# First input tile in halves on two queues, alternating loads, delayed products: a start-up change to a linear-attention kernel

## The chip, the cores and the metric

One core of one Trainium2 chip. The metric is the device time of one execution in microseconds (us). Several executions of each kernel are run and the median is quoted. The profile's span is about 2 us shorter than the time and comes from one execution.

The engines in the profile: PE is the TensorE matmul, PEld its weight load, DVE is VectorE, ACT is ScalarE, POOL is GpSimd, SP is SyncE. SP and ACT each own a DMA queue here.

## The reference

Two linear-attention blocks A and B read the same input x (2048 rows, 640 columns, bf16), each with its own weights, and a gate per row mixes their results.

```
g = sigmoid((x * gate_w).sum(-1))
q, k, v = split(x @ wqkv)              # 32 heads of 20
phi = lambda t: where(t > 0, t + 1, exp(t)) + 1e-6
kv = einsum(phi(k), v);  z = phi(k).sum(over rows)
o  = (phi(q) @ kv) / (phi(q) @ z + 1e-6)
block = o @ wo
out = g * block_A + (1 - g) * block_B
```

## The kernel before

The kernel is a list of operations that a small scheduler in Python orders on each engine, with a semaphore for each dependency. Four parts matter here. A "tile" is 128 rows of x; a "chunk" is 128 of the 640 rows of a weight matrix.

The loads that the first products need: input tiles 0 to 3 and the five chunks of A's key weights, 160 KB each.

```
load_wk("ACT", 0)
load_x("SP", 0)
load_wk("ACT", 1)
load_x("SP", 1)
load_wk("ACT", 2)
load_wk("SP", 3)
load_wk("ACT", 4)
load_x("SP", 2)
load_x("ACT", 3)
# ... then all else, on SP
```

The order on PE at the start. Everything up to the fourth block of key products is chained, so PE runs it in exactly this order. `warm` is a dummy matmul of 512 columns, `transpose_x(t)` is five PE transposes and one copy by DVE from PSUM to SBUF, and `first("A", (t, c))` is the two 320-column products of tile t with chunk c.

```
warm(7)
transpose_x(0)
warm(1)
transpose_x(1)
first("A", (0, 0), (0, 1))
warm(1)
first("A", (1, 0), (1, 1))
first("A", (0, 2), (1, 2), (0, 3), (1, 3))
transpose_x(2)
# ... (0, 4), (1, 4), transpose_x(3), then all of tiles 2 and 3
```

The middle: query products, with the small products `wp_unit("B", q)` (masked inner matrix times output weights) strewn between them. `wp_unit` needs a mask that DVE applies to the result of `m_unit`.

```
def queries(b):
    for X in XS:
        for k in range(NC):
            q_unit(X, b, k)
            if b == 1 and X == "A":
                wp_unit("B", k)
queries(0)
m_unit("B", 0)
m_unit("B", 1)
queries(1)
wp_unit("B", 5)
```

The denominators: DVE adds epsilon to them, then takes the reciprocal.

```
sch.op("DVE", lambda e: e.tensor_scalar(DN[...], PS[...], EPS, None, op0=ALU.add), ...)
```

Of the kernel before, what the change touches and what calls it, by code (L numbers as in the profile page):

```python
# [24 lines left out]
NC = 5  # L25
EPS = 1e-6
HALF = 320
XW = 672
PE_GHZ = 2.4

# [276 lines left out]
def _dve_ns(n, rate=1):  # L307
    return n / (0.96 * rate) + 68.0
# [6 lines left out]
def bass_gated_mix__linear_attn_block__linear_attn_block__prompt_kernel(nc, A_x, A_wqkv, A_wo, B_x, B_wqkv, B_wo, gate_w, out):  # L315
# [6 lines left out]
    with ExitStack() as es:  # L322
        E = es.enter_context

        def sb(name, shape, dtype=dt.bfloat16):
            return E(nc.sbuf_tensor(name, shape, dtype))
# [24 lines left out]
        GWB = sb("GWB", [128, D])  # L351
        NTS = 3
        TS = sb("TS", [128, NTS, D], dt.float32)
        DN = sb("DN", [128, 2, 256], dt.float32)
        RC = sb("RC", [128, 2, 256])
        RX = sb("RX", [128, 2, 1024])
# [32 lines left out]
        def mms(name, steps, reads, writes, cols, lat=190.0, par=1, prio=None, after=None):  # L389


            def fn(pe):
                ins = None
                for o, l, r, a, z, tp in steps():
                    ins = pe.matmul(o, l, r, start=a, stop=z, tile_position=tp, skip_group_check=True)  # L395
                return ins

            return sch.op("PE", fn, cols / PE_GHZ / par, reads=reads, writes=writes, name=name, lat=lat, prio=prio, after=after)
# [5 lines left out]
            return weights(X, lo, 0, NC)  # L404


        sch.op("POOL", lambda e: e.memset(IDN[:, :], 0.0), 150, writes=[("ID",)], name="id0")
        sch.op(
            "POOL",
# [8 lines left out]
        def load_x(eng, t):  # L418
            dma(eng, "xn%d" % t, XN[:, t, 0:D], xin[128 * t : 128 * t + 128, :], writes=[("XN", t)], us=0.25)

        def load_wk(eng, c):
            dma(eng, "wkA%d" % c, WK["A"][:, c, :], weights("A", D, c, c + 1)[:, 0, :], writes=[("WK", "A", c)], us=0.25)

        load_wk("ACT", 0)
        load_x("SP", 0)
        load_wk("ACT", 1)
        load_x("SP", 1)
        load_wk("ACT", 2)
        load_wk("SP", 3)
        load_wk("ACT", 4)  # L430
        load_x("SP", 2)
        load_x("ACT", 3)
        for c0, c1 in ((0, 1), (1, 3), (3, 5)):
            dma(
                "SP", "wkB%d" % c0, WK["B"][:, c0:c1, :], weights("B", D, c0, c1), writes=[("WK", "B", c) for c in range(c0, c1)],
# [38 lines left out]
        def transpose_x(t):  # L474
            tt = _Tile(1)

            def fn(pe):
                ins = None
                for c in range(NC):
                    ins = pe.transpose(PSB[:, tt.banks[0], 128 * c : 128 * c + 128], XN[:, t, 128 * c : 128 * c + 128], IDN[:, :])  # L480
                return ins

            at[0] = sch.op(
                "PE", fn, 5 * 112, reads=[("XN", t), ("ID",)], writes=[(tt,)], name="xpose%d" % t, lat=190, after=at[0]
            )
            sch.op(
                "DVE",
                lambda e: e.tensor_copy(
                    XT[:, :, 128 * t : 128 * t + 128], PSB[:, tt.banks[0], 0:D].rearrange("p (c f) -> p c f", f=128)
                ),  # L490
                _dve_ns(D), reads=[(tt,)], writes=[("XT", t)], name="xev%d" % t,
            )

        ring = {"ek": _Ring(NEK), "dn": _Ring(2), "rx": _Ring(2), "os": _Ring(NOS), "ts": _Ring(NTS)}

# [26 lines left out]
        def k_part(X, t, tile, cs, chain=False):  # L522
            xc = slice(128 * t, 128 * t + 128)
            order = [(h, c) for h in (0, 1) for c in cs] if len(cs) == NC else [(h, c) for c in cs for h in (0, 1)]

            def steps():
                return [
                    (PS[:, tile.banks[h], 0:HALF], XT[:, c, xc], WK[X][:, c, HALF * h : HALF * h + HALF], c == 0, c == NC - 1, None)
                    for h, c in order
                ]  # L530

            o = mms(
                "k%s%d_%d" % (X, t, cs[0]), steps, [("XT", t)] + [("WK", X, c) for c in cs], [(tile,)], len(cs) * (D + 12),
                after=at[0] if chain else None,
            )
            if chain:
                at[0] = o
# [142 lines left out]
        def q_unit(X, b, k):  # L680
            tile = _Tile(1)
            es = _Tile(1, ring["ek"])

            def ek():
                return EK[:, es.slot, 0:512]

            dst = PQ[X][:, k, 512 * b : 512 * b + 512]
            span = range(S * k + 512 * b, S * k + 512 * b + 512)
            over = [("F", X, "k", t) for t in range(span[0] // D, span[-1] // D + 1)]

            def steps():
                return [
                    (PS[:, tile.banks[0], :], WQ[X][:, c, k : D : NC], XT[:, c, 512 * b : 512 * b + 512], c == 0, c == NC - 1, None)
                    for c in range(NC)
                ]

            mms("q%s%d%d" % (X, b, k), steps, [("XT", t) for t in range(4 * b, 4 * b + 4)] + [("WQ", X)], [(tile,)], NC * 518, after=gone[X])
            sch.op(
                "ACT", lambda e: e.activation(ek(), PS[:, tile.banks[0], :], ACT.Exp), _act_ns(512), reads=[(tile,)],  # L699
                writes=[(es,)], name="eq%s%d%d" % (X, b, k),  # L700
            )
            sch.op(
                "DVE", lambda e: e.tensor_scalar(ek(), ek(), 1.0, EPS, op0=ALU.min, op1=ALU.add), _dve_ns(512, 4),  # L703
                reads=[(es,)], writes=[(es,)], name="tq%s%d%d" % (X, b, k),
            )
            sch.op(
                "DVE",
                lambda e: e.scalar_tensor_tensor(  # L708
                    out=dst, in0=PS[:, tile.banks[0], :], scalar=0.0, in1=ek(), op0=ALU.max, op1=ALU.add
                ),  # L710
                _dve_ns(512), reads=[(tile,), (es,)], writes=[("PQ", X, k, b)] + over, name="sq%s%d%d" % (X, b, k),
            )
# [24 lines left out]
        def scale_q(b, dtile, pieces):  # L737

            ds = _Tile(1, ring["dn"])
            lo = 256 * (b % 2)  # L740
            sch.op(
                "DVE",
                lambda e: e.tensor_scalar(DN[:, ds.slot, :], PS[:, dtile.banks[0], lo : lo + 256], EPS, None, op0=ALU.add), _dve_ns(256),
                reads=[(dtile,)], writes=[(ds,)], name="dn%d" % b,
            )

            def rec(e):
                with nc.allow_low_precision(reason="the factor is a bf16 matmul operand"):
                    return e.reciprocal(RC[:, ds.slot, :], DN[:, ds.slot, :])

            sch.op("DVE", rec, 1740, reads=[(ds,)], writes=[(ds,)], name="rc%d" % b)
            rep = FD[b].ap()
            dma(
                "SP", "fw%d" % b, rep.rearrange("g h r f -> (g h) r f"), lambda: RC[:, ds.slot, :].unsqueeze(1).to_broadcast([128, 4, 256]),
                reads=[(ds,)], writes=[("FD", b)], us=0.6,
            )
            xs = _Tile(1, ring["rx"])
            dma(
                "SP", "fr%d" % b, lambda: RX[:, xs.slot, :].rearrange("p (g f) -> p g f", f=256), rep.rearrange("g h r f -> (h r) g f"),
                reads=[("FD", b)], writes=[(xs,)], us=0.6,  # L760
            )
            w = 512 // pieces
            for j in range(pieces):
                for x, X in enumerate(XS):
                    def fn(e, j=j, x=x, X=X):
                        v = PQ[X][:, :, 512 * b + w * j : 512 * b + w * j + w]
                        return e.tensor_tensor(
                            out=v, in0=v, in1=RX[:, xs.slot, 512 * x + w * j : 512 * x + w * j + w].unsqueeze(1).to_broadcast([128, NC, w]), op=ALU.mult
                        )
                    ts = range(4 * b + 4 * j // pieces, 4 * b + 4 * (j + 1) // pieces)  # L770
                    sch.op(
                        "DVE", fn, _dve_ns(NC * w, 2), reads=[(xs,)] + [("PQ", X, k, b) for k in range(NC)],
                        writes=[("PQS", X, t) for t in ts], name="ml%s%d" % (X, b),
                    )
# [62 lines left out]
        def first(X, *tc):  # L837
            for t, c in tc:
                k_part(X, t, kt[X, t], [c], chain=True)

        warm(7)
        transpose_x(0)
        warm(1)
        transpose_x(1)
        first("A", (0, 0), (0, 1))
        warm(1)
        first("A", (1, 0), (1, 1))
        first("A", (0, 2), (1, 2), (0, 3), (1, 3))
# [36 lines left out]
        def queries(b):  # L885
            for X in XS:
                for k in range(NC):
                    q_unit(X, b, k)
                    if b == 1 and X == "A":
                        wp_unit("B", k)  # L890

        def finals(b):
            for t in range(4 * b, 4 * b + 4):
# [6 lines left out]
        m_unit("B", 0)  # L900
        m_unit("B", 1)
        queries(1)
        wp_unit("B", 5)
        wp_rows("B")
        d01 = dens(0)
        scale_q(0, d01, 2)
# [44 lines left out]
```

## Time and profile before

| | before |
|---|---|
| median time, first three runs | 194.16 us (194.12 to 194.65) |
| profile span | 192.3 us |
| PE busy | 187.7 us, 98% |
| third tile's products start | 8.90 us |
| last matmul starts | 189.48 us |

From the profile page before, the busy time of each engine and the chain of work that ended last:

```profile
PE 187.7 (98%) x1318; PEld 132.8 (69%) x1323; DVE 129.6 (67%) x249; ACT 73.6 (38%) x112; POOL 2.7 (1%) x12
...
PE 93%; DMA 3%; DVE 1%; ACT 1%; ACTq 0%; issue 0%
PE ps L395 93%; DMA WKA<-in_A_wqkv_dram 3%; DVE MB L607 1%; ACTq L384 0%; DVE FEB L708 0%; PE ps L480 0%; ACT EK L699 0%; ACT TS L815 0%; DVE OL L821 0%; DVE EK L703 0%
```

The chain is PE nearly throughout, so only time in which PE stands idle, or works in vain, can be won. The timeline view gives PE's groups of instructions with their start, their length and the idle time before them. At the start, the kernel before:

```profile
3.71 0.45 PE L480 MATMUL ps<-IDN,XN 128*128 128x128 bf16 x5
4.00 0.38 PE L395 MATMUL ps<-const-bfloat16-1.0 128*128 128x512 bf16 x1
4.40 0.45 PE L480 MATMUL ps<-IDN,XN 128*128 128x128 bf16 x5
4.75 0.72 PE L395 MATMUL ps<-WKA,XT 128*128 128x320 bf16 x4
...
5.53 0.71 PE L395 MATMUL ps<-WKA,XT 128*128 128x320 bf16 x4
6.58 1.26 PE L395 MATMUL ps<-WKA,XT 128*128 128x320 bf16 x8 [0.35 <-DMA WKA<-in_A_wqkv_dram]
...
8.62 0.45 PE L480 MATMUL ps<-IDN,XN 128*128 128x128 bf16 x5
8.90 0.57 PE L395 MATMUL ps<-WKA,XT 128*128 128x320 bf16 x3
```

Here the two transposes are the lines from L480, and the products with `WKA` wait at 6.58 for a weight chunk. That is chunk 2, the third DMA of ACT's queue. In the middle, the same view:

```profile
108.30 0.44 PE L395 MATMUL ps<-GTB,WVB 128*128 128x120 bf16 x8
108.81 1.03 PE L395 MATMUL ps<-XT,WQA 128*128 128x512 bf16 x4
110.44 0.48 PE L395 MATMUL ps<-WOB,MB 120*120 120x320 bf16 x2 [0.61 <-DVE MB L607]
```

The w-products of B (`WOB,MB`) waited for the masks on DVE. The line says 0.61 us.

### The profile page before, as it was taken

Reading aid. Unit: us, or ns where it says so; the run is one execution under the profiler, and the core shown is the slowest. Engines: PE = TensorE matmul, PEld = TensorE weight load, DVE = VectorE, ACT = ScalarE, POOL = GpSimd, SP = SyncE. Lnnn points to the kernel's source line nnn. Section 1 sums busy time; section 2 is a strip of 40 time slices with the busy share of each in tenths; the row PEclk is TensorE's granted clock in tenths of the full one; section 3 lists DMA queues with packets and bytes.
Section 4 is the critical chain, followed back from the end, with each engine's and each line's share of the span. In section 5 each row is a group of like instructions: output and inputs, shape, how many; then the busy total and the mean of one; then the engine's idle time right before and its main releaser. Section 6 shows DMA issues by size and latency. Waiting matters only on the chain.

```text
span 192.3 us, 3194 instructions
## 1 busy us (share of the span) xinstructions
PE 187.7 (98%) x1318; PEld 132.8 (69%) x1323; DVE 129.6 (67%) x249; ACT 73.6 (38%) x112; POOL 2.7 (1%) x12
## 2 busy tenths in 40 slices
PE   8999999999999999999999899999999999999994
PEld 3677777777888888988855565555556677777773
DVE  1298888888600019994179968899999987933323
ACT  2245454545211121103265377635553312332232
POOL 5000000000000000000000000000000000000000
DMA  6999899995011511121155303263200136211112
GB/s 196 306 205 191 176 388 234 291 226 156 3 34 34 38 34 34 38 34 34 34 112 131 137 0 83 91 203 113 74 0 3 55 116 186 102 68 38 68 68 68
DMA packets 30609, 21.17 MB, mean 110 GB/s; under 512 B 15492, under 2 KB 30340, under 8 KB 30596
## 3 DMA queue, kind: packets, MB, share of 16 engines
q1 hardware_dynamic: 29876, 20.16, 41.6%
q10 hardware_dynamic: 720, 0.82, 1.3%
q8 instruction: 10, 0.16, 0.4%
q14 instruction: 3, 0.02, 0.0%
HBM read 12.06 MB, written 5.31 MB: 90 GB/s over the span
## 4 chain that ended last, share of the span: by engine, by line
PE 93%; DMA 3%; DVE 1%; ACT 1%; ACTq 0%; issue 0%
PE ps L395 93%; DMA WKA<-in_A_wqkv_dram 3%; DVE MB L607 1%; ACTq L384 0%; DVE FEB L708 0%; PE ps L480 0%; ACT EK L699 0%; ACT TS L815 0%; DVE OL L821 0%; DVE EK L703 0%
## 5 line engine op out<-in xcount | busy, mean ns | idle before, releaser
L699 ACT ACTIVATE EK<-ps 128x512 bf16<-128x512 f32 x40 | 23.9, 597 | 20.1 <-PE ps L395 19.6
L506 ACT ACTIVATE EK<-ps 128x640 bf16<-128x640 f32 x32 | 22.4, 703 | 23.8 <-PE ps L395 23.8
L815 ACT ACTIVATE TS<-ps,GA 128x640 f32<-128x640 f32 (+2 forms) x18 | 13.2, 734 | 31.0 <-PE ps L395 31.0
L395 PE MATMUL ps<-WPB,FEB 128*128 128x320 bf16 (+1 forms) x165 | 24.7, 295 | 0.0
L395 PE MATMUL ps<-WPA,FEA 128*128 128x320 bf16 (+1 forms) x165 | 24.7, 295 | 0.0
L395 PE MATMUL ps<-WKA,XT 128*128 128x320 bf16 x160 | 23.1, 299 | 0.3 <-DMA WKA<-in_A_wqkv_dram 0.3
L395 PE MATMUL ps<-XT,WQA 128*128 128x512 bf16 x96 | 22.5, 379 | 0.2
L395 PE MATMUL ps<-XN,FEB 128*128 128x320 bf16 (+1 forms) x160 | 22.5, 300 | 0.0
L395 PE MATMUL ps<-WKB,XT 128*128 128x320 bf16 x160 | 22.4, 299 | 0.0
L395 PE MATMUL ps<-XT,WQB 128*128 128x512 bf16 x99 | 22.2, 379 | 0.1
L395 PE MATMUL ps<-XN,FEA 128*128 128x320 bf16 (+1 forms) x160 | 22.0, 300 | 0.0
L821 DVE SCALAR_TENSOR_TENSOR OS<-ps,GA,TS 128x640 bf16<-128x640 f32 x15 | 13.0, 874 | 12.9 <-PE ps L395 11.4
L557 ACT ACTIVATE GS<-ps 128x640 bf16<-128x640 f32 x10 | 7.0, 703 | 37.1 <-PE ps L395 37.1
L395 PEld LDWEIGHTS ps<-XN,FEA 128*128 128x128 bf16 x160 | 18.8, 117 | 3.0
L395 PEld LDWEIGHTS ps<-XN,FEB 128*128 128x128 bf16 x160 | 18.7, 118 | 2.9
L395 PEld LDWEIGHTS ps<-WPA,FEA 128*128 128x128 bf16 x165 | 15.9, 98 | 6.1
L395 PEld LDWEIGHTS ps<-WPB,FEB 128*128 128x128 bf16 x165 | 15.8, 98 | 6.2 <-issue 0.4
L395 PEld LDWEIGHTS ps<-WKA,XT 128*128 128x128 bf16 x160 | 15.4, 98 | 6.6 <-DMA WKA<-in_A_wqkv_dram 0.7
L395 PEld LDWEIGHTS ps<-WKB,XT 128*128 128x128 bf16 x160 | 15.7, 98 | 6.1
L395 PEld LDWEIGHTS ps<-XT,WQB 128*128 128x128 bf16 x100 | 11.7, 117 | 9.7
L395 PEld LDWEIGHTS ps<-XT,WQA 128*128 128x128 bf16 x100 | 11.6, 118 | 8.8 <-issue 0.4
L661 DVE SCALAR_TENSOR_TENSOR GP<-XN,GWB 128x640 bf16<-128x640 bf16 x16 | 13.3, 833 | 4.1 <-PE ps L395 3.6
(52 smaller groups left out, 150.8 us busy)
## 6 DMA issues: line engine op xcount, KB each, us to landing
out_dram<-OS SPq DMA_DIRECT2D x15, 160.0 KB, 1.8
XN<-in_A_x_dram SPq DMA_DIRECT2D x3, 640.0 KB, 8.5
factor<-RC SPq DMA_DIRECT2D x4, 256.0 KB, 2.6
RX<-factor SPq DMA_DIRECT2D x4, 256.0 KB, 2.9
WVA<-in_A_wqkv_dram SPq DMA_DIRECT2D x1, 800.0 KB, 12.7
WQA<-in_A_wqkv_dram SPq DMA_DIRECT2D x1, 800.0 KB, 14.9
WVB<-in_B_wqkv_dram SPq DMA_DIRECT2D x1, 800.0 KB, 17.0
WQB<-in_B_wqkv_dram SPq DMA_DIRECT2D x1, 800.0 KB, 15.6
```

Source lines behind the costliest of these rows:

```text
L395: ins = pe.matmul(o, l, r, start=a, stop=z, tile_position=tp, skip_group_check=True)
L506: "ACT", lambda e: e.activation(ek2(), pair(tile, HALF), ACT.Exp),
L557: "ACT", lambda e: e.activation(GS[:, k, :].rearrange("p (h f) -> p h f", f=HALF), pair(tile, HALF), ACT.Copy),
L607: return e.tensor_tensor(out=MB[0:n, qq[0] : qq[-1] + 1, 0:n].rearrange("p q (i k) -> p q k i", k=NC), in0=PS[0:n, tile.banks[0], at : at ...
L661: lambda e, t=t: e.scalar_tensor_tensor(out=GP[:, :], in0=XN[:, t, 0:D], scalar=1.0, in1=GWB[:, :], op0=ALU.mult, op1=ALU.mult, accum_out= ...
L699: "ACT", lambda e: e.activation(ek(), PS[:, tile.banks[0], :], ACT.Exp), _act_ns(512), reads=[(tile,)],
L815: "ACT", lambda e, acc=acc, t_ap=t_ap: e.activation(t_ap(), acc(), ACT.Copy, scale=GA[:, 0, t : t + 1]),
L821: lambda e, acc=acc, t_ap=t_ap, o_ap=o_ap: e.scalar_tensor_tensor(out=o_ap(), in0=acc(), scalar=GA[:, 1, t : t + 1], in1=t_ap(), op0=ALU.m ...
```

## The change

Its intent: get the first transpose going earlier, feed both queues evenly, keep the weight chunks from trailing the input tiles, hide the mask wait, and take four small operations off DVE. The diff, cut to its core:

```diff
+WPLAG = 2
...
+        for eng, h in (("SP", 0), ("ACT", 1)):
+            dma(eng, "xn0_%d" % h, XN[:, 0, HALF * h : HALF * h + HALF], xin[0:128, HALF * h : HALF * h + HALF], ...)
         load_wk("ACT", 0)
-        load_x("SP", 0)
-        load_wk("ACT", 1)
-        load_x("SP", 1)
-        load_wk("ACT", 2)
-        load_wk("SP", 3)
-        load_wk("ACT", 4)
-        load_x("SP", 2)
-        load_x("ACT", 3)
+        load_wk("SP", 1)
+        load_x("ACT", 1)
+        load_wk("SP", 2)
+        load_wk("ACT", 3)
+        load_wk("SP", 4)
+        load_x("ACT", 2)
+        load_x("SP", 3)
...
-            (one DVE copy of the five transposed blocks)
+            for c0, c1 in ((0, 2), (2, NC)) if t < 2 else ((0, NC),):
+                (a DVE copy of blocks c0 to c1)
...
-                "DVE", lambda e: e.tensor_scalar(DN[...], PS[...], EPS, None, op0=ALU.add), ...
+                "ACT", lambda e: e.activation(DN[...], PS[...], ACT.Identity, bias=EP[:, 0:1]), ...
...
-        warm(7)
+        warm(6)
         transpose_x(0)
         warm(1)
+        first("A", (0, 0), (0, 1))
         transpose_x(1)
-        first("A", (0, 0), (0, 1))
         warm(1)
         first("A", (1, 0), (1, 1))
...
-                    if b == 1 and X == "A":
-                        wp_unit("B", k)
+                    q = 5 * (X == "B") + k - WPLAG
+                    if b == 1 and 0 <= q < 6:
+                        wp_unit("B", q)
...
         queries(1)
-        wp_unit("B", 5)
```

More of the change, by code (lines that the diff above doesn't have):

```diff
@@ L353, in bass_gated_mix__linear_attn_block__linear_attn_block__prompt_kernel @@
         TS = sb("TS", [128, NTS, D], dt.float32)
+        EP = sb("EP", [128, 1], dt.float32)
         DN = sb("DN", [128, 2, 256], dt.float32)
@@ L404, in wsrc @@
             return weights(X, lo, 0, NC)
+        sch.op("POOL", lambda e: e.memset(EP[:, :], EPS), 100, writes=[("EP",)], name="ep")
         sch.op("POOL", lambda e: e.memset(IDN[:, :], 0.0), 150, writes=[("ID",)], name="id0")
@@ L422, in load_wk @@
             dma(eng, "wkA%d" % c, WK["A"][:, c, :], weights("A", D, c, c + 1)[:, 0, :], writes=[("WK", "A", c)], us=0.25)
-        load_wk("ACT", 0)
-        load_x("SP", 0)
-        load_wk("ACT", 1)
-        load_x("SP", 1)
-        load_wk("ACT", 2)
-        load_wk("SP", 3)
-        load_wk("ACT", 4)
-        load_x("SP", 2)
-        load_x("ACT", 3)
+        for eng, h in (("SP", 0), ("ACT", 1)):
+            dma(
+                eng, "xn0_%d" % h, XN[:, 0, HALF * h : HALF * h + HALF], xin[0:128, HALF * h : HALF * h + HALF],
+                writes=[("XN0", h)], us=0.15,
+            )
+        load_wk("ACT", 0)
+        load_wk("SP", 1)
[5 more added lines that the diff above has]
+        load_x("SP", 3)
         for c0, c1 in ((0, 1), (1, 3), (3, 5)):
@@ L483, in transpose_x @@
             at[0] = sch.op(
-                "PE", fn, 5 * 112, reads=[("XN", t), ("ID",)], writes=[(tt,)], name="xpose%d" % t, lat=190, after=at[0]
+                "PE", fn, 5 * 112, reads=[("XN", t), ("ID",)] + [("XN0", h) for h in (0, 1)][: 2 - 2 * min(t, 1)], writes=[(tt,)], name="xpose%d" % t, lat=190, after=at[0]
             )
-            sch.op(
-                "DVE",
-                lambda e: e.tensor_copy(
-                    XT[:, :, 128 * t : 128 * t + 128], PSB[:, tt.banks[0], 0:D].rearrange("p (c f) -> p c f", f=128)
-                ),
-                _dve_ns(D), reads=[(tt,)], writes=[("XT", t)], name="xev%d" % t,
-            )
+            for c0, c1 in ((0, 2), (2, NC)) if t < 2 else ((0, NC),):
+                sch.op(
+                    "DVE",
+                    lambda e, c0=c0, c1=c1: e.tensor_copy(
+                        XT[:, c0:c1, 128 * t : 128 * t + 128],
+                        PSB[:, tt.banks[0], 128 * c0 : 128 * c1].rearrange("p (c f) -> p c f", f=128),
+                    ),
+                    _dve_ns(128 * (c1 - c0)), reads=[(tt,)], writes=[("XTC", t, c) for c in range(c0, c1)], name="xev%d" % t,
+                )
         ring = {"ek": _Ring(NEK), "dn": _Ring(2), "rx": _Ring(2), "os": _Ring(NOS), "ts": _Ring(NTS)}
@@ L532, in k_part @@
             o = mms(
-                "k%s%d_%d" % (X, t, cs[0]), steps, [("XT", t)] + [("WK", X, c) for c in cs], [(tile,)], len(cs) * (D + 12),
+                "k%s%d_%d" % (X, t, cs[0]), steps, ([("XTC", t, c) for c in cs] if t < 4 else [("XT", t)]) + [("WK", X, c) for c in cs], [(tile,)], len(cs) * (D + 12),
                 after=at[0] if chain else None,
@@ L695, in steps @@
                 ]
-            mms("q%s%d%d" % (X, b, k), steps, [("XT", t) for t in range(4 * b, 4 * b + 4)] + [("WQ", X)], [(tile,)], NC * 518, after=gone[X])
+            mms("q%s%d%d" % (X, b, k), steps, ([("XT", t) for t in range(4 * b, 4 * b + 4)] if b else [("XTC", t, c) for t in range(4) for c in range(NC)]) + [("WQ", X)], [(tile,)], NC * 518, after=gone[X])
             sch.op(
@@ L741, in scale_q @@
             sch.op(
-                "DVE",
-                lambda e: e.tensor_scalar(DN[:, ds.slot, :], PS[:, dtile.banks[0], lo : lo + 256], EPS, None, op0=ALU.add), _dve_ns(256),
-                reads=[(dtile,)], writes=[(ds,)], name="dn%d" % b,
+                "ACT",
+                lambda e: e.activation(DN[:, ds.slot, :], PS[:, dtile.banks[0], lo : lo + 256], ACT.Identity, bias=EP[:, 0:1]), _act_ns(256),
+                reads=[(dtile,), ("EP",)], writes=[(ds,)], name="dn%d" % b,
             )
```

## The prediction

> **What bounds the kernel now.** TensorE. The chain of waits gives it 93% of the 192.3 us span, a DMA 3%. By stretch, PE is busy 87.50 of 87.50 us (9.0 to 96.5) and 44.80 of 44.80 us (144.7 to 189.5); the granted clock is 1.00. A 320-column matmul starts every 136 ns, so a busy array leaves nothing to win, and the change touches no large matmul. By the timeline, PE loses time in three places:
> 1. The start. Useful matmuls become gapless at 6.58 us, when the third weight chunk has landed (the chain charges 4.89 us to it); a small gap (0.12 us) waits at 8.62 for the fourth input tile.
> 2. 110.44 us: the first w-product of B waits for the masks on DVE; the groups say 0.61 us idle.
> 3. The tail, about 2.5 us after the last matmul, which the change leaves alone.
>
> **What the change does.**
> - *Input tile 0 in halves, one per queue.* Today it lands 2.9 us after issue, at 3.64 us, beside a weight chunk. Halves bring 160 KB instead of 320 KB before the first transpose. DMA moves 350 to 400 GB/s at 2.5 to 4 us, so about 0.4 us earlier: 3.25. One cold warm-up matmul (427 ns) less makes PE free at 3.34. The Trainium skill (DMA: Bandwidth & Descriptors, Issuing engines are not separate DMA queues) says that all queues share the same engines; the trace agrees, as the sum stays at 320 to 400 GB/s with both active. Alternating changes order, not rate.
> - *Split eviction.* The 0.49 us copy becomes about 0.25 + 0.3. Products of tile 0 should begin near 4.3 instead of 4.75 us.
> - *New order of loads.* Input tile 1 moves from second on its queue (landed 4.36) to third, behind five tiles of bytes: I expect 5.2 us. After it come its transpose, eviction and two first products: 0.8 + 0.55 us more of PE work behind the wait than today. Products of chunk 2 start near 6.4 rather than 6.58; the gap at 8.62 goes. Net gain 0.3 us, uncertain from -0.8 to +0.8. Break-even is tile 1 landing at about 5.35 us; today the third DMA of the ACT queue landed only at 6.55.
> - *w-products of B two query units later* (1.08 us each): the first issues near 111.0, after its mask (110.4). This removes 0.55 us of wait in full, as PE has query matmuls meanwhile.
> - *Adding epsilon moves from DVE to ACT* (four of 0.41 us). DVE is at 90% at 125 to 150 us, but PE doesn't wait there; the first final tile (144.8) follows its scaling (136.4) by 8 us: worth nothing. The Trainium skill (ScalarE: Activation LUTs, Table sets) says identity is in every set, so I expect still one table load of 1.28 us.
>
> **Sum.** 0.55 us in the middle, 0.3 us at the start: 194.16 - 0.85 = 193.3 us, 0.4% faster. Range 192.6 to 194.4. Faster by over 2%: 0.01; within 2%: 0.98; slower by over 2%: 0.01.
>
> **What would show it.** First transpose at 3.35 us (now 3.71); first product at 4.3 (now 4.75); PE's last wait before the long run is for the second tile's eviction near 5.9; products of the third tile start near 8.6 (now 8.90); idle before the w-products of B goes from 0.61 to about 0; four 128x256 activations of about 0.4 us replace DVE's; the last matmul ends 0.85 us earlier.
>
> **What would make it wrong.** Tile 1 landing late (a straggling DMA engine, as the chunk at 6.55 us shows), which delays everything behind it, since the order on PE is fixed; rows of 640 bytes moving no faster than full ones; a second table load; a changed order in the middle that opens a new wait.

## The result, and the profile after

| | before | after |
|---|---|---|
| median of 6 runs each, same rounds | 194.41 us | 193.65 us |
| ratio of the fast runs | | 0.9963 (95%: 0.9941 to 0.9985) |
| both again in a later series | 194.28 us (11 runs) | 193.95 us (6 runs) |
| ratio there | | 0.9997 (0.9970 to 1.0025) |
| profile span | 192.3 us | 192.1 us |
| third tile's products start | 8.90 us | 9.27 us |
| last matmul starts | 189.48 us | 189.03 us |

A ratio is the mean time of one kernel's fast runs over that of the other's in the same rounds, so it is not quite the ratio of the medians. The change is faster by some tenths of a us, or by nothing that can be told from noise, depending on the rounds.

The page after, the same two parts:

```profile
PE 188.3 (98%) x1322; PEld 133.3 (69%) x1322; DVE 128.2 (67%) x247; ACT 75.4 (39%) x116; POOL 2.8 (1%) x13
...
PE 98%; DVE 0%; ACT 0%; issue 0%
PE ps L397 97%; PE ps L487 1%; ACT TS L824 0%; DVE OL L830 0%; DVE XT L496 0%
```

The DMA has left the chain. That looks like a start that waits no more, but it is not. Here is the timeline of the start after the change:

```profile
3.29 0.74 PE L487 MATMUL ps<-IDN,XN 128*128 128x128 bf16 x5
3.82 0.63 PE L397 MATMUL ps<-const-bfloat16-1.0 128*128 128x512 bf16 x1
4.41 1.25 PE L397 MATMUL ps<-WKA,XT 128*128 128x320 bf16 x4
5.61 0.53 PE L487 MATMUL ps<-IDN,XN 128*128 128x128 bf16 x5
5.98 0.38 PE L397 MATMUL ps<-const-bfloat16-1.0 128*128 128x512 bf16 x1
6.53 1.80 PE L397 MATMUL ps<-WKA,XT 128*128 128x320 bf16 x12 [0.17 <-DVE XT L496]
...
8.99 0.44 PE L487 MATMUL ps<-IDN,XN 128*128 128x128 bf16 x5
9.27 0.30 PE L397 MATMUL ps<-WKA,XT 128*128 128x320 bf16 x1
```

The reader is to see four things.
- The first transposes start at 3.29 instead of 3.71 us and the first product at 4.41 instead of 4.75, as intended.
- The second tile's transposes start at 5.61 instead of 4.40.
- After them PE has nothing real to do until the copy is done, at 6.53.
- The third tile's products start 0.37 us later than before.

Why 5.61? The view of DMAs, cut to the moment 1.75 us, shows the two DMAs being issued then, the third of each queue, with the KB of each and the us from issue to landing. Before:

```profile
WKA<-in_A_wqkv_dram SPq DMA_DIRECT2D x1, 160.0 KB, 3.5
WKA<-in_A_wqkv_dram ACTq DMA_DIRECT2D x1, 160.0 KB, 4.9
```

After:

```profile
WKA<-in_A_wqkv_dram SPq DMA_DIRECT2D x1, 160.0 KB, 3.7
XN<-in_A_x_dram ACTq DMA_DIRECT2D x1, 160.0 KB, 3.9
```

What stands third on ACT's queue is now the input tile `XN` (tile 1). It was issued at 1.65 and its semaphore was complete at 5.56. In the waits view after, two lines tell of it:

```profile
PEld ps L397 <- DVE XT L496: 1.0, 2, 0.5
...
PEld ps L487 <- DMA XN<-in_A_x_dram: 0.5, 1, 0.5
```

So weight loads waited 0.5 us for the tile and 1.0 us for two copies. (That is no loss by itself: before, weight loads waited 1.3 us for input tiles. The order in the timeline shows the loss.) The chain on the page shows no DMA because the products before the transposes ran at half rate up to just before the landing: four products at 4.41, 4.65, 4.92 and 5.19 us, up to 267 ns apart where 136 is usual. The chain follows PE's own work through this stretch, and that work was merely slow enough to fill the wait. The last of the four would have let go of PE at 5.45 (5.19 plus 267 ns), so in this trace PE itself stood still for the late tile for only 0.16 us.

The middle went the other way. Busy time by engine in the stretch from the first query products to the first denominators, before and after. The columns are the stretch, its length, then busy us and instructions of PE, PEld, DVE, ACT and POOL, the clock, the DMA share and GB/s:

```profile
96.50:124.10 27.60, 26.81 (x150) 15.64 (x150) 22.83 (x48) 17.07 (x29) 0.00 (x0) 1.00 0.35 96
```

```profile
96.87:123.65 26.78, 26.78 (x153) 15.72 (x150) 22.65 (x48) 16.96 (x29) 0.00 (x0) 1.00 0.36 99
```

The stretch became 0.82 us shorter, and PE is now busy in all of it. The 0.79 us that it was not busy before (27.60 less 26.81) should not be taken too exactly: three matmul records are missing there (150 against 153), which counts as idle, and the modelled ends of matmuls hide some idle time. The length of the stretch has neither fault. The groups by form show that the wait is gone, before and after:

```profile
L395 PE MATMUL ps<-WOB,MB 120*120 120x320 bf16 x12 | 2.7, 303 | 0.6 <-DVE MB L607 0.6
```

```profile
L397 PE MATMUL ps<-WOB,MB 120*120 120x320 bf16 x12 | 2.6, 300 | 0.0
```

In the timeline after, 15 query products now stand where 5 stood (4 of the 5 are on record), and the w-products follow them without a wait:

```profile
108.95 3.41 PE L397 MATMUL ps<-XT,WQA 128*128 128x512 bf16 x15
112.20 0.44 PE L397 MATMUL ps<-WOB,MB 120*120 120x320 bf16 x2
```

From the start of the third tile's products to the start of the last matmul takes 180.58 us before and 179.76 after, 0.82 less. The start lost 0.37, so the last matmul starts 0.45 us earlier. That stretch will serve as a measure in what follows: in every trace of this case it is 180.57 to 180.59 us without the delay of the w-products and 179.76 us with it, whatever else was changed.

### The profile page after: what moved, and what is told of

It reads as the page before. It is cut to its first block, busy times and chain, and to the rows that moved or that the text cites. A ratio compares the mean times of both kernels' runs of the same rounds, so it can differ in the third digit from the quotient of the medians.

```text
span 192.1 us, 3201 instructions
## 1 busy us (share of the span) xinstructions
PE 188.3 (98%) x1322; PEld 133.3 (69%) x1322; DVE 128.2 (67%) x247; ACT 75.4 (39%) x116; POOL 2.8 (1%) x13
## 4 chain that ended last, share of the span: by engine, by line
PE 98%; DVE 0%; ACT 0%; issue 0%
PE ps L397 97%; PE ps L487 1%; ACT TS L824 0%; DVE OL L830 0%; DVE XT L496 0%
## 5 line engine op out<-in xcount | busy, mean ns | idle before, releaser
L397 PE MATMUL ps<-XT,WQB 128*128 128x512 bf16 x100 | 22.7, 379 | 0.0
```

The source lines that it names most:

```text
L397: ins = pe.matmul(o, l, r, start=a, stop=z, tile_position=tp, skip_group_check=True)
```

## The experiments

Two theories stood after the comparison. A: the delay of the w-products is worth 0.8 us, and the start of the change loses, because input tile 1 now lands late and its transpose and copy stand bare in front of PE. B, as predicted: 0.55 us in the middle plus a gain at the start; the late start in one profile is an unlucky draw. A third, C, put the loss at the start on the clock: PE reached its full rate at 3.7 us in the trace before and at 5.8 in the trace after.

### The parts alone

The w-products' delay alone:

```diff
 (kernel before)
-                    if b == 1 and X == "A":
-                        wp_unit("B", k)
+                    q = 5 * (X == "B") + k - WPLAG
+                    if b == 1 and 0 <= q < 6:
+                        wp_unit("B", q)
-        wp_unit("B", 5)
```

> The kernel before with one part of the change: the w-products of B two query units later. Theory A (my reading of the two traces): this part alone is worth the 0.77 us by which consecutive matmul starts exceed their cadence at 109.46 us of the trace before (985 ns instead of 216), so the time is 0.75 to 0.8 us under the kernel before of the same rounds, more than the whole change gave. Rival B: the gain of the whole change (0.72 us in the mean) is made of 0.55 here, as predicted, plus a gain at the start; then this run is only about 0.5 us faster. In the profile under both: no matmul gap over 100 ns between 96 and 123 us.

Measured: 193.38 us against 194.22, ratio 0.9950 (0.9916 to 0.9983). Its trace takes 179.76 us from the third tile's products to the last matmul, the same as the whole change. Its timeline in the middle:

```profile
108.27 3.19 PE L396 MATMUL ps<-XT,WQA 128*128 128x512 bf16 x14
111.29 0.44 PE L396 MATMUL ps<-WOB,MB 120*120 120x320 bf16 x2
111.56 0.81 PE L396 MATMUL ps<-XT,WQA 128*128 128x512 bf16 x3
```

The w-products now stand where no wait is noted before them. It was run again later, on the same chip with other versions beside it:

> The w-product delay alone, a second time. Theory A: 0.6 to 1.0 us faster than the kernel before, as in its first run (0.84 by the medians, ratio 0.995); the stretch from the third tile's products to the last matmul is 179.76 us, where the kernel before has 180.58. Rival: the first run was a lucky draw of starts and the gain is 0.3 us, like the changed kernel's second run.

Measured: 193.27 against 194.19, ratio 0.9946 (0.9916 to 0.9977), and 179.76 us for the same stretch. In the mean the delay alone gave more than the whole change (its intervals and those of the whole change overlap). By time alone 0.55 us would still be possible; what lets B fall is the trace: the stretch is 0.82 us shorter, not 0.55, and the delay's two starts (8.36 and 8.47 us) were earlier than the changed kernel's (9.27).

The start alone (the loads, the split copies, the order on PE and 6 warm-ups of the change; the rest as before):

```diff
 (changed kernel)
-WPLAG = 2
-                    q = 5 * (X == "B") + k - WPLAG
-                    if b == 1 and 0 <= q < 6:
-                        wp_unit("B", q)
+                    if b == 1 and X == "A":
+                        wp_unit("B", k)
-  epsilon on ACT
+  epsilon on DVE
```

> The kernel before with only the start of the change: input tile 0 in halves, the alternating loads, the split copies, tile 1 transposed after the first products, 6 warm-up matmuls. Theory A: a loss. The third tile's products started 0.37 us later after the change (9.27 against 8.90), so this is 0.1 to 0.4 us slower than the kernel before. Rival B (the prediction): 0.3 us faster. In the profile under A: the second tile's transpose waits for its DMA, which lands at about 5.5 us, and the gap of about 0.77 us before the w-products of B is back.

Measured: 194.84 against 194.22, ratio 1.0032 (0.9997 to 1.0067), so 0.6 us slower in the mean, more than the 0.1 to 0.4 expected, with an interval that just reaches "no change". The mechanism is as A has it. Its waits, the lines of PE that answer to the question:

```profile
PEld ps L395 <- DVE XT L493: 1.4, 2, 0.9
...
PE ps L395 <- DVE MB L613: 0.6, 1, 0.6
...
PEld ps L484 <- DMA XN<-in_A_x_dram: 0.5, 1, 0.5
```

Tile 1 landed at 5.89, the third tile's products began at 9.61, and the mask wait was back with its 0.61 us. One trace is one draw, but the draws don't overlap: with the old loads and the old order on PE those products began at 8.36 to 9.11 us (before, the delay twice, epsilon), with the change's start at 9.27 to 9.77 (the change twice, this run).

The addition of epsilon alone on ACT:

```diff
-                "DVE", lambda e: e.tensor_scalar(DN[...], PS[...], EPS, None, op0=ALU.add)
+                "ACT", lambda e: e.activation(DN[...], PS[...], ACT.Identity, bias=EP[:, 0:1])
```

> The kernel before with only the addition of epsilon moved from DVE to ACT. Theory: nothing, within 0.1 us of the kernel before, as matmuls run at their cadence throughout 122 to 189 us in the trace before. Rival: it shortens a wait that the trace hides and gives 0.2 us or more. In the profile: four ACT instructions of about 0.45 us, one table load, first matmul of the finals at the same time to 0.1 us.

Measured: 194.11 against 194.22, ratio 0.9989 (0.9958 to 1.0020); 180.59 us from the third tile's products to the last matmul, against 180.58. It is worth nothing that shows, though DVE does less. The three parts sum to -0.0050 + 0.0032 - 0.0011 = -0.0029 of the time, between the two measurements of the whole (-0.0037 and -0.0003); each of these figures is uncertain by about 0.003.

### What in the start costs

One more warm-up in the changed kernel, for theory C:

```diff
-        warm(6)
+        warm(7)
```

> The changed kernel with 7 warm-up matmuls again instead of 6. Theory A (late second input tile): the start waits for the tile that lands at about 5.5 us, so one warm-up more costs nothing and gains nothing: within 0.1 us of the changed kernel. Rival C (cold clock): the start lost because the array ran at half rate until 5.6 us instead of 3.7 us (a 320-column product every 267 ns instead of 136), and 7 warm-ups end that earlier: 0.3 us faster than the changed kernel. If the clock's switch is set by something that doesn't depend on the program, its time varies from run to run in all profiles.

Measured: ratio to the kernel before 1.0000 (0.9957 to 1.0044); no gain, so C is not supported, though the interval is too wide to exclude 0.3 us. Its profiled run was a slow one (196.54 us, clock 0.991). In its trace tile 1 landed only at 6.84, PE stood idle for 1.33 us before it, and from 7.88 to 10.55 us products were 267 ns apart again. The switch to full rate does vary from run to run. In the five traces with the old loads and 7 warm-ups (before, the delay twice, epsilon, and a version below) the first full-rate matmul stands at 3.7, 3.8, 4.1, 6.0 and 4.6 us. So a switch as late as 5.8 is met without the change too. But in all five traces with tile 0 in halves and 6 warm-ups no matmul ran fully at full rate before 5.8 us (with 7, in the slow run's trace, one did at 4.8), so a link with the change is not excluded. And the slow clock had a part in the start: see the end of this section.

Input tile 1 later still, fourth on its queue:

```diff
-        load_x("ACT", 1)
-        load_wk("SP", 2)
-        load_wk("ACT", 3)
+        load_wk("ACT", 3)
+        load_wk("SP", 2)
+        load_x("ACT", 1)
```

> The changed kernel with input tile 1 one place later still, fourth on the ACT queue behind weight chunk 3. Theory A (the landing of input tile 1 sets the start after the change): it lands near 6.8 us instead of 5.6, the third tile's products follow 3.7 us later, and the kernel is 0.7 to 1.5 us slower than the changed one, more where the idle array falls back to half rate. Rival (the start is bound by the total of bytes, whose order does not matter): no slower than the changed kernel.

Measured: 194.97 against 194.19, ratio 1.0057 (1.0012 to 1.0101). Against the changed kernel (0.9963 and 0.9997) that is 0.6 to 0.9% or 1.2 to 1.8 us more. Two of its six runs (196.54 and 196.88 us) show a clock of 0.991, as the slow run above did, though they count as fast. Without them the mean is 194.74 us against 194.25 before, and by the ratios 0.5 to 1.2 us more than the changed kernel is left. Its timeline:

```profile
7.17 0.45 PE L487 MATMUL ps<-IDN,XN 128*128 128x128 bf16 x5 [1.35 <-DMA XN<-in_A_x_dram]
...
8.01 1.80 PE L397 MATMUL ps<-WKA,XT 128*128 128x320 bf16 x12 [0.17 <-DVE XT L496]
...
10.76 0.43 PE L397 MATMUL ps<-WKA,XT 128*128 128x320 bf16 x2
```

The tile landed at 7.13, and PE waited for it. The third tile's products follow the transposes by 3.58 us here, by 3.66 after the change, by 3.67 with the start alone: what comes after these transposes is fixed, and where the tile comes late enough, its landing moves it all. This is the strongest evidence for A.

The start of the change with the old loads:

```diff
 (start alone)
-  the loads of the change
+  the loads of before (tile 0 whole)
```

> The start of the change with the old loads: split copies, tile 1 transposed after the first products of tile 0, 6 warm-ups, but input tile 0 whole and the loads in their old order; nothing else of the change. Theory A (the new place of input tile 1 in the loads is what costs): this is within 0.15 us of the kernel before, since its start waits for the third DMA of the ACT queue (a weight chunk) as before. Rival (the split copies or the new order on the array cost): as slow as the whole start, 0.4 to 0.6 us slower than before. In the profile under A: the third tile's products follow that chunk's landing by about 2.4 us, as before, not by 3.7.

Measured: 194.38 against 194.28, ratio 1.0020 (0.9995 to 1.0046). By time this can't be told from nothing or from half of the start's loss. The profile went against my expectation: tile 1 had landed at 4.49, but its transposes came at 5.46, behind the first products, and the products of tile 1 at 6.29, 0.7 us after chunk 2 had landed at 5.58. The third tile's products came 3.45 us after chunk 2's landing, not 2.4, and 3.57 us after the transposes of tile 1, as in the others. So in this trace the new order on PE has a price of its own even when the tile is there. For comparison, in the first trace of the delay alone, with the old order, chunk 2 landed about as early (5.63) and the third tile's products began at 8.36, not 9.03. In the old order the copy of tile 1 (4.89 to 5.38 us before) ran while PE did tile 0's first products (4.75 to 5.3); in the new one PE waits for it.

Tile 1 and chunk 1 change places, and tile 1 is transposed before chunk 1's products:

```diff
 (start alone)
-        load_wk("SP", 1)
+        load_x("SP", 1)
-        load_x("ACT", 1)
+        load_wk("ACT", 1)
-        first("A", (0, 0), (0, 1))
+        first("A", (0, 0))
         transpose_x(1)
         warm(1)
-        first("A", (1, 0), (1, 1))
+        first("A", (1, 0), (0, 1), (1, 1))
```

> The start of the change with one pair exchanged: input tile 1 is second on the SP queue and weight chunk 1 third on the ACT queue, and tile 1 is transposed before chunk 1's products. Everything else as in the run of the start alone (0.62 us slower than before). Theory A: what then waits for the third DMA of ACT has 2.7 us of work behind it up to the third tile's products instead of 3.7, so it is 0.4 to 1.0 us faster than the start alone, about 0.3 us faster than or equal to the kernel before; input tile 1 lands near 4.2 us, chunk 1 near 5.7. Rival (halves and alternation as such cost): no better than the start alone.

Measured: 194.20 against 194.28, ratio 1.0002 (0.9979 to 1.0024). That is 0.6 us better than the start alone by the ratios, which come from different chips and have overlapping intervals, and no better than before. By time, halves and alternation as such cost nothing that shows. The trace doesn't confirm it: tile 1 landed at 4.67 rather than 4.2, and the third tile's products began at 9.34, no earlier than after the change. PE ran at half rate until 6.2 us in this execution.

The second trace of the changed kernel (its times are at the end of the next section) shows that the landing of tile 1 doesn't always decide. Its start:

```profile
5.08 1.23 PE L397 MATMUL ps<-WKA,XT 128*128 128x320 bf16 x4 [0.62 <-DMA WKA<-in_A_wqkv_dram]
6.09 0.55 PE L487 MATMUL ps<-IDN,XN 128*128 128x128 bf16 x5
...
7.03 1.80 PE L397 MATMUL ps<-WKA,XT 128*128 128x320 bf16 x12 [0.17 <-DVE XT L496]
```

Tile 1 had landed at 5.72. But chunk 0 had landed only at 4.94, the first products ran at half rate, 267 ns apart, up to 6.09, and the transposes came right behind them. At 136 ns each the products would have ended near 5.6 (an estimate from these starts). So here the late chunk and the slow clock held the start, and the transposes with their copies stood bare behind them all the same.

### Versions meant to beat both

The delay with both input tiles first, one on each queue, then chunks 0 to 4 alternating:

```diff
 (delay alone)
+        load_x("SP", 0);  load_x("ACT", 1)
+        load_wk("SP", 0); load_wk("ACT", 1); load_wk("SP", 2); load_wk("ACT", 3); load_wk("SP", 4)
+        load_x("ACT", 2); load_x("SP", 3)
-        first("A", (0, 0), (0, 1))
         warm(1)
-        first("A", (1, 0), (1, 1))
+        first("A", (0, 0), (1, 0), (0, 1), (1, 1))
```

> A version meant to beat both: the w-products of B delayed, and input tiles 0 and 1 whole, first on each queue, then chunks 0 to 4 alternating, then tiles 2 and 3; both tiles transposed before any product. Theory A: both tiles land by about 3.9 us, products begin at about 4.7 and follow the chunks without a long wait; third tile's products at 8.0 to 8.4 us against 8.90, so 1.2 to 1.7 us faster than the kernel before and at least as fast as the w-product delay alone (193.38). Rival (the last chunks land no earlier in any order, at 6.9 to 7.7 us): no faster than the w-product delay alone, 0.8 us under the kernel before.

Measured: 193.35 against 194.28, ratio 0.9954 (0.9931 to 0.9978). It is no better than the delay alone. Products began at 5.63, not 4.7: two dummy matmuls at half rate (427 ns each) stood in the way. Without those:

```diff
-        warm(7)
+        warm(6)
         transpose_x(0)
-        warm(1)
         transpose_x(1)
-        warm(1)
```

> The version with both input tiles first, without the two dummy matmuls between the transposes and the products and with 6 warm-ups. Theory: in its run with them the dummies ran at half rate (427 ns each) in the way of the transposes, and products began only at 5.63 us; now they begin near 4.9. If that was what held it, it is 0.3 to 0.6 us faster than with them. Rival: tile 2 landing at about 7.8 us plus 1.0 us of transpose and copy bounds the start, so the third tile's products still begin at 8.7 to 9.0 and nothing is gained.

Measured: 193.16 against 194.19, ratio 0.9942 (0.9912 to 0.9971). Products began at 4.96 as intended, but the third tile's began at 9.27: tile 2 landed at 8.11 and its transposes started at 8.15. The rival holds in this trace, and by time nothing is gained over the version with the dummies.

The delay with chunk 3 ahead of chunk 2:

```diff
-        first("A", (0, 2), (1, 2), (0, 3), (1, 3))
+        first("A", (0, 3), (1, 3), (0, 2), (1, 2))
```

> The w-product delay with the old start, in which the products of weight chunk 3 go ahead of those of chunk 2: in all four traces with the old loads chunk 3 lands 0.25 to 1.35 us earlier. Theory: the 0.5 us in which the array waited for chunk 2 in the trace before is filled with four matmuls (0.54 us), so 0.0 to 0.5 us faster than the delay alone, 0.8 to 1.3 us faster than the kernel before. Rival: the start is bound by the last loads (tiles 2 and 3 and chunk 4), and this gives nothing over the delay alone. The runs scatter by 0.5 us, so the profile decides: third tile's products less than 2.3 us after chunk 2's landing under the theory.

Measured: 193.55 against 194.19, ratio 0.9962 (0.9930 to 0.9994). This is inconclusive: in its profile chunk 2 landed at 5.57, before PE came to want it, so there was no wait to fill. The third tile's products came 2.96 us after that landing, and my mark of 2.3 us was missed.

Last, the changed kernel again beside these:

> The changed kernel once more, to stand on the same chip and rounds as the others. Theory A: 0.2 to 0.7 us faster than the kernel before, slower than the w-product delay alone was (0.84 us by the medians). Its profile shows, in the stretch from the third tile's products to the last matmul, 179.8 us as before; its start is another draw of landing time of input tile 1 (5.5 to 6.9 us) and of the clock's switch to full rate.

Measured: 193.95 against 194.28, ratio 0.9997 (0.9970 to 1.0025), with 179.76 us from the third tile's products to the last matmul and a start that brought those products only at 9.77. By the ratio (under 0.1 us) it fell short of my range, 0.2 to 0.7 us; by the medians (0.33 us) it lay inside.

The best version is the kernel before with the delay alone, or with both tiles first: 0.9942 to 0.9954 in four series. The intervals overlap with that of the changed kernel's first series; what makes me prefer it is the trace, where the long stretch is equal and the start is earlier (8.36 and 8.47 us for the delay alone, against 9.27 and 9.77). With both tiles first the start was no earlier in its two traces (9.01 and 9.27), so for that version only the times speak.

## Why the prediction was right or wrong

The time lay inside the range (193.65 against 193.3, 192.6 to 194.4), and the forecast of 0.4% was near to 0.37% measured. Yet two of its terms were wrong, and the errors partly cancelled: in the traces the last matmul starts 0.45 us earlier (0.82 less 0.37), not 0.85. That the times of the first series came so near to the forecast is partly luck; the later series gave 0.03%.

1. *"Net gain 0.3 us" at the start*: wrong in sign. The start lost 0.37 us in the profile and 0.6 in the mean of the start alone. The step that failed is the path through tile 1: landing at 5.2 us, worked out from the bytes ahead of it, and chunk 2's products from 6.4. Measured: 5.56 and 7.08, so the tile came later than predicted, and the way behind it took 1.52 us instead of 1.2. (The prediction's own terms, 5.2 + 0.8 + 0.55, give 6.55 and not 6.4.)

   The 0.68 us between 6.4 and 7.08 divide so in the trace: PE was busy with half-rate products until 5.45, which the prediction left out (0.25); it then stood for the tile until 5.61 (0.16); and from these transposes to chunk 2 took 1.47 us instead of 1.2 (0.27), since tile 1's products waited 0.92 us for its transposes and copies with nothing else to do. Had the tile landed at 5.2, PE would still have come to it at 5.45, and by this account the start would have lost about 0.2 us (an estimate from these starts).

   The landing itself was misjudged too. What I took as the exception, the third DMA of ACT's queue landing as late as 6.55, was not rare: in the traces of all 14 versions and repeats that DMA, whatever it carries, landed between 5.45 and 7.25 us, six times after 6.4 and never by the break-even of 5.35.

   Compared with before, tile 1's transposes started 1.21 us later (5.61 against 4.40), the work and waits from there to the third tile's products shrank from 4.51 to 3.66 us, and the difference is the loss. The old order needed less luck: tile 1's copy ran beside tile 0's products, and what arrived late was a chunk with less work behind it.
2. *"This removes 0.55 us of wait in full"*: the mechanism was right, the size was off. It measured 0.82 us. Two misreadings made it small. The idle time of 0.61 counts from the modelled end of the last matmul, 379 ns after its start, while the next one could have started after 216. That hides 0.16 us, and the wait is 0.77. I then took a further part of the gap for a missing record. A record is missing, but elsewhere: PE shows four query products at 108.81 where PEld shows five weight loads from 108.56. The remaining 0.05 us is the first w-product's slow start (184 ns instead of 136).
3. *Tile 0 in halves and the split copies*: right where they act. The first transposes came at 3.29 (predicted 3.35), the first product at 4.41 (predicted 4.3). PE won 0.34 us there and lost it in front of tile 1. But the halves stand before chunk 0 in the queues, and that chunk landed later with them (4.28 to 4.94 us, against 3.84 to 4.02 with the old loads). In the start alone and in the second trace of the change the first product came only at 4.8 and 5.08, later than before.
4. *Alternating changes order, not rate*: nothing here contradicts it. The Trainium skill says that DMAs of all issuing engines run on the same 16 DMA engines and interleave (DMA: Bandwidth & Descriptors, Issuing engines are not separate DMA queues). The later one of tiles 2 and 3, the last of these loads, landed at 7.69 to 8.21 us in the four traces with the change's loads, and at 7.52 to 8.71 in the six with the old ones: no difference that shows.
5. *Epsilon on ACT is worth nothing, one table load*: right. The experiment gave 0.9989 with an interval around 1. After the change the profile has four activations of 474 ns, and one table load of 1283 ns, as the Trainium skill's remark that identity is in every set led me to expect (ScalarE: Activation LUTs, Table sets).
6. *What would make it wrong*: tile 1 landing late was named as the first risk and happened; the half-rate products and the copies that nothing covered were not named.

What stays open: why the third DMA of a queue lands anywhere between 5.45 and 7.25 us, how the loss of the start divides between the loads, the order on PE and the slow clock (by time 1.0020 and 1.0032 can't be told apart, and in the traces it differs from run to run), and what fixes the moment of the clock's switch.

## What to carry to other kernels

Before a load is moved back in a queue, ask how much work stands behind it and nowhere else to be done: a late load with 3.7 us of chained work behind it costs more than one with 2.4. Ask too what runs beside the transposes and copies that feed the next products: in the new order nothing did. Judge a gap on PE by the distance of matmul starts, not by the idle time before an instruction. And test each part of a combined change alone: here one part carried all of the gain, another gave part of it back, and the sum looked like a forecast come true.

## What the Trainium skill lacked or had wrong

- TensorE: Matmul & The Clock Gate (What you observe) puts the switch to full rate around 4 us into sustained matmul activity, give or take 0.5 us from run to run. With the first matmul at 0.77 us and hardly a pause on PE, the first full-rate matmul stood at 3.7 us in the trace before and at 6.0 in the trace of epsilon alone: 2.9 and 5.2 us into the activity (dummy matmuls, transposes and products together), a wider spread. In other traces it stood later still, but after pauses of PE, and so they say less.
- DMA: Bandwidth & Descriptors has no figure for how unevenly the 16 parts of one copy arrive. In the trace before, 13 of the 16 increments of chunk 2's semaphore had come by 5.44 us and the last three at 5.63, 5.95 and 6.53, so one part delayed the whole by more than 0.5 us.
- Perfetto Trace Analysis warns that matmul busy time is a bad measure of the distance to roofline as matmuls are pipelined, but does not say that the idle time shown in front of a matmul is too small for the same reason: 0.61 us was shown where 0.77 were lost.
